# Attention and a two-layer expert on one core: expert products as three fp16 products instead of three fp32r products

## The chip, the cores and the metric

One NeuronCore of a Trainium2 chip runs the whole program. The metric is device microseconds of one execution, the median over runs. Its engines are called PE (TensorE, matmuls), DVE (VectorE), ACT (ScalarE), POOL (GpSimd) and SP (SyncE, which here issues every DMA). PEld is the weight load of a matmul, which overlaps PE.

## The reference

The program computes attention with a gated memory, and puts the result through an expert of two matrices. B, H, S, D are 4, 8, 576, 64; the expert is 512 by 2048 and back, for 2304 tokens.

```python
scores = scale * np.matmul(q, k.transpose(0, 1, 3, 2))      # causal mask, softmax -> a
local = np.matmul(a, v)
q_p = phi(q)                                                # elu + 1
mem_out = einsum(q_p, M_prev) / (einsum(q_p, z_prev)[..., None] + 1e-06)
attn = g * mem_out + (1 - g) * local                        # g = sigmoid(beta)
x = attn.transpose(0, 2, 1, 3).reshape(B * S, H * D)
h = x @ w_in                                                # w_in, w_out are float64
g = h * np.cos(h)
return (g @ w_out).astype(np.float32)
```

## The kernel before

**Tokens.** The 2304 tokens are nine chunks of 256. Chunk 0 is the first 64 rows of all four batches; its attention is done in four small pieces (`small_pair`). The rest comes in five attention jobs (`prm["jobs"]`): row blocks 1 and 2 of batch 0, row blocks 3 and 4 of batch 0, then all four row blocks of batches 1, 2 and 3. A job runs over four pairs of heads (`heads`), and fills `x`, one tile of 128 by 512 for each row block. While a job runs, the expert works on the chunks that earlier jobs finished (`moe_chunk`). The last two chunks are left when attention ends.

**Attention.** For a pair of heads PE makes the scores (`scores`, L540, fp32, in two halves of the array), DVE takes them from PSUM with mask and row minimum (`least`, L551), ACT takes the exponential with its sum (`expo`, L558). Then the weights of the softmax have to be turned. In all jobs but the first `parts` does so: ACT or DVE writes an fp16 high part (L363 or L365, both are the helper `copy`), DVE an fp16 rest (L570), SP issues a DMA transpose (L574), and the product with the values (`local`, L712) is fp16: 3r+2 matmuls of 64 columns for row block r. For this the values are scaled to a power of two and split (`values`, L615 to L627 and the helpers). In the first job `plain` is set: PE turns the softmax in fp32 (`turned`, L585 and L587), one copy takes it from PSUM, and the product is fp32 (L703).

**Expert.** A chunk has eight units. `unit1` makes 256 columns of h for 256 tokens (tile `u`), `hidden` makes g from them, `unit2` adds their share to two accumulators `acc`. In chunk 0 all of it is fp32 (`split` is false). In the other eight chunks x, g and both matrices are each the sum of an fp32r high part and an fp32r rest (`xh`, `xl`, `gh`, `gl`, `weight_high`, `weight_low`, or both in one tile, `wide_both`), and a product is three products: a `unit1` of 24 matmuls of 256 columns (L914), a `unit2` of 12 matmuls of 512 columns (L958). `emit_xT` turns x with four PE transposes for each of two tiles (L886); ACT rounds the high part out of PSUM (L897), DVE subtracts the rest. `hidden` is a chain ACT (L937), DVE (L939), ACT sine (L941), DVE (L943), ACT `gh` (L363), POOL or DVE `gl` (helper `sub`, L373).

**Weights.** `load_w` rebuilds a float32 tile from the two halves of float64 with POOL, ACT and DVE steps. When chunk 0 has used a tile for the last time, `split_w` splits it: ACT the high part (L504), DVE the rest (L511).

**Order.** Nothing runs in the order in which it is written. Each step is an `Op` with the engines that may do it, a cost, and a priority in `prm`; `Plan.forward` gives every engine one list of steps from these numbers, and the program holds each engine's steps in that order. There is one PSUM bank `mm` (transposes, memory products and sums of values share it), two for `S`, `u` and `acc` each, one for `pv`. A `w` tile has two buffers; two `s` tiles for each row block hold the softmax of the two heads of a pair.

Of the kernel before, what the change touches and what calls it, by code (L numbers as in the profile page):

```python
# [275 lines left out]
def dve(n, wide=False):  # L276
    return 65 + n / (1.92 if wide else 0.96)
# [15 lines left out]
def kernel(  # L293
# [33 lines left out]
    gate = sb.tile([128, 6, H], F32, name="gate")  # L327
    ig, il, ils = gate[:, 3, :], gate[:, 4, :], gate[:, 5, :]
# [161 lines left out]

    def split_w(key, prio, used):
        if len(w_split) >= prm["wide"] and wide:
            ph = pl = wide.pop(0)
        else:
            ph, pl = [(places or last).pop(0) for part in range(2)]
# [12 lines left out]
        def low(e):
            if ph != pl:
                wl[key] = sb.tile([128, 512], F32R, tag=pl, name=f"{pl}_low")  # L510
            eng[e].tensor_tensor(out=wl[key], in0=wv[key], in1=wh[key].bitcast(F32), op=ALU.subtract)  # L511

        o = Pp(some({"ACT": act(512, False), "DVE": dve(512, True), "Pool": pool(512)}, "hi_on"), high, prio,
               after=[w_ready[key], *left_by.get(ph, list)()])
        w_ready[key] = Pp(some({"DVE": dve(512), "Pool": 1240}, "lo_on"), low, prio, after=[o, *left_by.get(pl, list)()])
        w_split.append(key)
        done = [*used, w_ready[key]]
        left_by[w_place[key]] = lambda: done
        places.append(w_place[key])
# [652 lines left out]
```

## Time and profile before

| | |
|---|---|
| runs | 579.73 us median of 3 (579.24 to 580.37) |
| span of the profiled execution | 578.5 us |
| PE, PEld busy | 98%, 81% |
| DVE, ACT, POOL busy | 70%, 70%, 28% |
| chain that ended last | PE 81% of it, ACT 7%, DMA 5%, DVE 3% |

The profiled execution's time is its span of 578.5 us; the median of the runs is 1.2 us above it. A matmul's record is longer than its place on PE, because matmuls are pipelined: what one costs is the distance from its start to the next one's, which is read from a row of several that follow each other.

### The profile page before, as it was taken

The numbers are of one execution on the slowest core, as the hardware profiler recorded it, in microseconds if no ns is written. First come the engines' busy times: TensorE is split into PE (matmuls) and PEld (weight loads), VectorE is DVE, ScalarE is ACT, GpSimd is POOL, SyncE is SP. The second block draws the span as 40 slices with busy tenths as digits, with TensorE's granted clock in tenths as the row PEclk, the third lists the DMA queues.
The fourth block names the chain that finished last, engine by engine and source line by source line (L and its number), as shares of the span: only waits on it lengthen the run. The fifth ranks groups of instructions, "written<-read, shape, count | busy, mean of one in ns | idle before, by whom it ended". The sixth has DMA issues, their size and how long they took to land.

```text
span 578.5 us, 12276 instructions
## 1 busy us (share of the span) xinstructions
PE 567.5 (98%) x4453; PEld 468.6 (81%) x4453; DVE 402.3 (70%) x1292; ACT 407.2 (70%) x872; POOL 160.1 (28%) x159
## 2 busy tenths in 40 slices
PE   8899999999999999999999999999999999999997
PEld 5677657688888788788977988888879999989995
DVE  4999788989989899889758855868698421321320
ACT  4997788898898897769657946968788532433432
POOL 2232330145225213115140311441213112222112
PEclk9999999999999999999999999999999999999999
DMA  8877773696644985485509810727056100000101
GB/s 277 286 228 236 241 231 98 122 200 139 140 97 99 182 160 114 92 168 143 81 0 191 168 31 1 164 76 150 1 103 125 31 1 19 19 0 1 38 0 37
DMA packets 113165, 64.96 MB, mean 112 GB/s; under 512 B 95952, under 2 KB 101584, under 8 KB 113104
## 3 DMA queue, kind: packets, MB, share of 16 engines
q1 hardware_dynamic: 113104, 64.18, 46.7%
q8 instruction: 35, 0.57, 0.4%
q14 instruction: 26, 0.21, 0.1%
HBM read 36.37 MB, written 4.72 MB: 71 GB/s over the span
## 4 chain that ended last, share of the span: by engine, by line
PE 81%; ACT 7%; DMA 5%; DVE 3%; issue 2%; SPq 1%; POOL 0%; ACTq 0%; POOLq 0%; DVEq 0%
PE u L914 32%; PE acc L958 31%; PE S L540 7%; PE pv L712 5%; DMA t<-p 2%; PE pv L703 2%; PE mm L669 2%; ACT s L558 2%; PE mm L886 1%; DMA ws<-in_w_in 1%; DVE p L570 1%; DMA q<-in_qk 1%; SPq L379 1%; ACT p L363 1%; ACT x L689 1%
## 5 line engine op out<-in xcount | busy, mean ns | idle before, releaser
L373 POOL TENSOR_TENSOR gl<-w,gh 128x512 fp32r<-128x512 f32 x64 | 84.7, 1325 | 249.7 <-ACT gh L363 175.2
L914 PE MATMUL u<-xh,weight_high 128*128 128x256 f32 x416 | 119.4, 287 | 1.0 <-DVE w L943 1.0
L914 PE MATMUL u<-xl,weight_high 128*128 128x256 f32 x416 | 115.9, 279 | 0.0
L914 PE MATMUL u<-xh,weight_low 128*128 128x256 f32 x416 | 115.7, 278 | 0.0
L939 DVE SCALAR_TENSOR_TENSOR w<-w,u 128x512 f32<-128x512 int32 x72 | 49.1, 684 | 84.7 <-ACT w L937 68.3
L958 PE MATMUL acc<-weight_high,gh 128*128 128x512 f32 x240 | 97.8, 407 | 0.0
L958 PE MATMUL acc<-weight_low,gh 128*128 128x512 f32 x240 | 94.4, 393 | 0.0
L958 PE MATMUL acc<-weight_high,gl 128*128 128x512 f32 x240 | 94.1, 392 | 0.0
L570 DVE SCALAR_TENSOR_TENSOR p<-s,p 128x64 f16<-128x64 f32 (+1 forms) x224 | 83.1, 414 | 6.2 <-ACT p L363 5.6
L914 PEld LDWEIGHTS u<-xh,weight_high 128*128 128x128 f32 x416 | 78.3, 188 | 6.5 <-issue 2.5
L558 ACT ACTIVATE s<-s,nb 128x448 f32<-128x448 f32 (+3 forms) x128 | 77.6, 610 | 5.9 <-DVE nb L551 5.6
L914 PEld LDWEIGHTS u<-xl,weight_high 128*128 128x128 f32 x416 | 78.3, 188 | 1.4
L914 PEld LDWEIGHTS u<-xh,weight_low 128*128 128x128 f32 x416 | 78.5, 189 | 0.0
L937 ACT ACTIVATE w<-u 128x512 int32<-128x512 f32 x72 | 42.4, 592 | 47.3 <-PE u L914 28.0
L363 ACT ACTIVATE gh<-w 128x512 fp32r<-128x512 f32 x56 | 35.2, 628 | 49.0 <-PE acc L958 40.6
L551 DVE CUSTOM_DVE_ANT_0 s<-S,mask 128x320 f32<-128x320 f32 (+3 forms) x128 | 65.5, 532 | 4.1 <-PE S L540 3.8
L943 DVE TENSOR_TENSOR w<-w,u 128x512 f32<-128x512 f32 x64 | 43.5, 683 | 22.4 <-ACT w L941 22.3
L540 PE MATMUL S<-stq 64*128 64x320 f32 (+4 forms) x320 | 55.6, 455 | 0.0
L941 ACT ACTIVATE w<-w 128x512 f32<-128x512 f32 x72 | 45.0, 629 | 14.8 <-DVE w L939 14.0
L958 PEld LDWEIGHTS acc<-weight_high,gh 128*128 128x128 f32 x240 | 45.1, 188 | 11.2 <-issue 2.7
L958 PEld LDWEIGHTS acc<-weight_low,gh 128*128 128x128 f32 x240 | 45.1, 188 | 10.1
L958 PEld LDWEIGHTS acc<-weight_high,gl 128*128 128x128 f32 x240 | 45.2, 188 | 7.5
(123 smaller groups left out, 1037.0 us busy)
## 6 DMA issues: line engine op xcount, KB each, us to landing
ws<-in_w_in SPq DMA_DIRECT2D x16, 512.0 KB, 5.4
ws<-in_w_out SPq DMA_DIRECT2D x16, 512.0 KB, 4.2
stq<-in_qkp SPq DMA_DIRECT2D x12, 544.0 KB, 4.2
stv<-in_vk SPq DMA_DIRECT2D x16, 320.0 KB, 3.3
out<-w SPq DMA_DIRECT2D x16, 256.0 KB, 2.2
t<-p SPq DMA_TRANSPOSE x112, 3.2
mz<-in_mzp SPq DMA_DIRECT2D x20, 66.0 KB, 2.6
stq<-in_qkp SPq DMA_DIRECT2D x4, 288.0 KB, 3.6
```

Source lines behind the costliest of these rows:

```text
L363: nc.scalar.activation(out=out, in_=in_, func=ACTF.Copy, scale=scale)
L373: lambda e: eng[e].tensor_tensor(out=out, in0=in0, in1=in1, op=ALU.subtract), prio, port=kw.pop('port', True), **kw)
L540: nc.tensor.matmul(out=sv.ap[:, c:c + n], lhsT=pair.ap[p, qs], rhs=pair.ap[p, k0:k0 + n], start=True, stop=True)
L551: return P.op({"DVE": dve(n) + 10}, lambda e: nc.vector.tensor_tensor_reduce(out=st.ap[:, k0:k0 + n], in0=sv.ap[:, c:c + n], in1=mk, scale ...
L558: return P.op({"ACT": act(W, False, 2)}, lambda e: nc.scalar.activation(out=st.ap[:, 0:W], in_=st.ap[:, 0:W], func=ACTF.Exp, scale=-1.0, b ...
L570: Pp({"DVE": dve(n)}, lambda e, c=c, n=n, to=to: nc.vector.scalar_tensor_tensor(out=pt.ap[:, to:to + n], in0=sa[:, c:c + n], scalar=PSCALE ...
L914: nc.tensor.matmul(out=u.ap[:, f, :], lhsT=a[:, cs:cs + 128], rhs=x, start=(n == 0), stop=(n == len(terms) - 1))
L937: P.op({"ACT": act(512)}, lambda e: nc.scalar.activation(out=wi, in_=u.ap, func=ACTF.Copy, bias=0.25), ep, r=[u], w=[w])
L939: P.op({"DVE": dve(512)}, lambda e: nc.vector.scalar_tensor_tensor(out=wv, in0=wi, scalar=0.25, in1=u.ap, op0=ALU.subtract, op1=ALU.subtra ...
L941: P.op({"ACT": act(512, False)}, lambda e: nc.scalar.activation(out=wv, in_=wv, func=ACTF.Sin, scale=-TWO_PI_BELOW), ep, w=[w], table="sin")
L943: P.op({"DVE": dve(512)}, lambda e: nc.vector.tensor_tensor(out=wv if split else views[0], in0=wv, in1=u.ap, op=ALU.mult), ep, r=[u], w=[w ...
L958: nc.tensor.matmul(out=acc[b].ap, lhsT=a, rhs=w, start=(i == 0 and f == 0 and n == 0), stop=(2 * i + f == NF - 1 and n == len(terms) - 1))
```

## The change

Five things change.

1. **Products.** x, g and both matrices are split into fp16 parts instead of fp32r parts, high and rest in one tile (`weight_both`). A product is still three products. In the program an fp16 matmul is a LDWEIGHTS and a MATMUL; an fp32r one is a MATMUL alone that loads its own weights.
2. **Scales.** fp16 needs scales. For each of eight groups of four weight tiles PE makes the Gram matrix of their upper halves (16 matmuls of 128 columns in bf16, read with a step of two), DVE takes its trace, PE adds it over partitions (one matmul of one column), DVE makes a power of two (`powers`). `factors` is run once when all eight are there. For x ACT takes sums of squares (one for each tile), PE adds them, DVE makes the scale. The scales enter as an operand per partition in `split_w`, in `hidden` and in `finish`.
3. **x.** No PE transposes for the eight split chunks. DVE scales x in place, ACT or DVE writes the fp16 high part, DVE or POOL the rest, SP issues one DMA transpose of eight 128 by 128 blocks for each tile.
4. **First job.** `plain` is 0: the first job goes through `values`, `parts` and the fp16 product as the others do.
5. **Order.** New costs and priorities in `prm` and in the `P.op` calls, hence a new order on all engines.

The counts of instructions that differ most, from the two programs:

| | before | after |
|---|---|---|
| expert products of split chunks | 1536 fp32r of 256 columns, 768 of 512 | 1536 fp16 of 256, 768 of 512 |
| first job's products with values | 40 fp32 | 104 fp16 |
| first job's PE transposes | 40 | 0 |
| PE transposes of x, split chunks | 64 | 0 |
| Gram matmuls; sums over partitions of one column | 0; 16 | 128; 44 |
| `gl` on POOL, on DVE | 64, 0 | 15, 49 |
| ACT table loads | 52 | 60 |
| DMA transposes of softmax, of x | 112, 0 | 128, 16 |
| instructions of DVE, ACT, POOL | 1294, 714, 164 | 1459, 782, 106 |

The diff, cut to its core:

```diff
+    def powers(prio, src, q, sc, r=(), a=(), after=()):
+        bank, xn = P.buf("mm"), P.buf("xn")
+        if r:
+            for b, x in enumerate(r):
+                def squares(e, x=x, to=xn.ap[:, b:b + 1]):
+                        nc.scalar.activation(out=junk_a, in_=x.ap, func=ACTF.Square, accum_out=to)
+        else:
+            def gram(e):
+                blocks = [x.bitcast(BF16)[:, 2 * c + 1:2 * c + 256:2] for x in src() for c in range(0, 512, 128)]
+                for n, x in enumerate(blocks):
+                    nc.tensor.matmul(out=bank.ap[:, 0:128], lhsT=x, rhs=x, start=(n == 0), stop=(n == len(blocks) - 1))
+            def trace(e):
+                    nc.vector.tensor_tensor_reduce(out=junk_d, in0=bank.ap[:, 0:128], in1=ident, scale=1.0,
+                                                   scalar=2.0**-100, op0=ALU.mult, op1=ALU.add, accum_out=xn.ap[:, 0:1])
+        def total(e):
+            for b in range(nb):
+                nc.tensor.matmul(out=bank.ap[:, 128:129], lhsT=ones.to_broadcast([128, 128]), rhs=xn.ap[:, b:b + 1],
+                                 start=(b == 0), stop=(b == nb - 1))
+        def go(e):
+            nc.vector.tensor_scalar(out=q.bitcast(I32), in0=bank.ap[:, 128:129].bitcast(I32), scalar1=1, scalar2=0x7F800000,
+                                    op0=ALU.logical_shift_right, op1=ALU.bitwise_and)
+            nc.vector.tensor_scalar(out=sc.bitcast(I32), in0=q.bitcast(I32), scalar1=-1, scalar2=204 << 23,
+                                    op0=ALU.mult, op1=ALU.add)
+    def factors(prio):
...
     def split_w(key, prio, used):
-                wh[key] = sb.tile([128, 512], F32R, tag=ph, name=f"{ph}_high")
-                nc.scalar.copy(out=wh[key], in_=wv[key])
-            eng[e].tensor_tensor(out=wl[key], in0=wv[key], in1=wh[key].bitcast(F32), op=ALU.subtract)
+            both = sb.tile([128, 1024], F16, tag=place, name=f"{place}_both")
+                nc.scalar.activation(out=wh[key], in_=wv[key], func=ACTF.Copy, scale=s)
+            eng[e].scalar_tensor_tensor(out=wl[key], in0=wv[key], scalar=s, in1=wh[key], op0=ALU.mult, op1=ALU.subtract)
...
     def emit_xT(prio, xbs, split):
-            bufs = [P.buf("xh"), P.buf("xl")]
+            xt, cs = P.buf("xT"), P.buf("cs")
+            o = powers(prio, None, cs.ap[:, 5:6], cs.ap[:, 6:7], r=xbs, a=[cs])
+                Pp({"DVE": dve(512, True, 1), "Pool": pool(512) + 65}, lambda e, xb=xb: eng[e].tensor_scalar(
+                    out=xb.ap, in0=xb.ap, scalar1=s, scalar2=1.0, op0=ALU.mult, op1=ALU.mult), prio, w=[xb], after=[o])
+                copy(hv, xb.ap, 512, prio, on=prm["xh_on"], r=[xb], w=[half])
+                sub(lv, xb.ap, hv, 512, prio, on=prm["xl_on"], r=[xb, half], w=[half])
+                P.op({"SP": 1200}, lambda e, b=b, half=half: nc.sync.dma_start_transpose(out=xt.ap[:, b], in_=half.ap), prio,
+                     r=[half], a=[xt], move=140.0 * 8, lead=-230.0)
...
     def hidden(ep, i, u, split, cs=None):
+            P.op({"ACT": act(512, extra=1)}, lambda e: nc.scalar.activation(
+                out=wi, in_=u.ap, func=ACTF.Copy, scale=d, bias=0.25), ep, r=[u, cs], w=[w])
+            P.op({"DVE": dve(512, extra=1)}, lambda e: nc.vector.scalar_tensor_tensor(
+                out=wv, in0=u.ap, scalar=d, in1=wi, op0=ALU.mult, op1=ALU.subtract), ep, r=[u, cs], w=[w])
+                out=wv, in_=wv, func=ACTF.Sin, scale=TWO_PI_BELOW, bias=quarter), ep, w=[w], table="sin", after=[o_const])
+                out=wv, in0=wv, scalar=ej, in1=u.ap, op0=ALU.mult, op1=ALU.mult), ep, r=[u], w=[w], after=w_fac)
...
-    "plain": 1,
+    "plain": 0,
-    "hi_on": ('ACT',),
-    "lo_on": ('DVE',),
+    "gram": 240.0,
```

How the new order moves things, at three places.

PE in chunk 0, the stretch in which it makes the first fp32 units and the first job's attention (`mm` is the shared bank, `s` a softmax tile, `t` a turned one, `stv` and `v` values). Before:

```order
L914 MATMUL u_129<-s_82,weight_val 128x256 x2
L914 MATMUL u_129<-s_86,weight_val 128x256 x2
L585 MATMUL mm_133<-ident,s_75 64x128
L587 MATMUL mm_133<-ident,s_75 128x128
...
L669 MATMUL mm_133<-mz_70,e_69 128x132 x2
L703 MATMUL pv_132<-stv_67,t_84 128x64 x3
L703 MATMUL pv_132<-stv_67,t_80 128x64 x2
L540 MATMUL S_130<-stq_65 128x320
```

After:

```order
L997 MATMUL u_142<-s_88,weight_val 128x256 x2
L997 MATMUL u_142<-s_92,weight_val 128x256 x2
L518 LDWEIGHTS weight_val
L518 MATMUL mm_146<-weight_val 128x128
...
L787 MATMUL pv_145<-v_78,t_82 128x64
L997 MATMUL u_141<-s_88,weight_val 128x256 x2
L997 MATMUL u_141<-s_92,weight_val 128x256 x2
L532 LDWEIGHTS ones
L532 MATMUL mm_146<-xn_118,ones 128x1
```

The transposes of the softmax and the fp32 products with values are gone; Gram products and sums over partitions stand between the fp32 units, and they use the bank `mm`.

DVE in the job of batch 1, around one unit of the expert. Before, where `gl` of the unit is on POOL's list:

```order
L939 SCALAR_TENSOR_TENSOR w_103<-w_103,u_129 128x512
L551 ISA s_78,nb_114<-S_130,mask 128x320
L551 ISA nb_114 128x1
L679 RECIPROCAL r_122<-r_122 128x4
L551 ISA s_74,nb_114<-S_130,mask 128x192
L551 ISA nb_114 128x1
L685 TENSOR_TENSOR x_98<-mm_133,r_122 128x128
L685 TENSOR_TENSOR x_99<-mm_133,r_122 128x128
```

After:

```order
L1024 SCALAR_TENSOR_TENSOR w_111<-u_142,cs_117,w_111 128x512
L1028 SCALAR_TENSOR_TENSOR w_110<-w_110,wfac,u_141 128x512
L620 ISA s_93,nb_127<-S_143,mask,nb_127 128x64
...
L620 ISA s_88,nb_128<-S_144,mask 128x448
L620 ISA nb_128 128x1
L380 TENSOR_TENSOR gl_114<-w_110,gh_112 128x512
L726 SCALAR_TENSOR_TENSOR e_75<-stq_71,e_75 128x512
```

`gl` has come onto DVE's list, among the scores of the next pair of heads, and both DVE steps of the unit read a scale per partition.

PE where the chunks of the last job begin. Before, PE turns x between products:

```order
L914 MATMUL u_128<-xl_101,wide_both 128x256
L914 MATMUL u_128<-xh_100,wide_both 128x256
L886 MATMUL mm_133<-ident,x_94 128x128 x4
L958 MATMUL acc_127<-weight_high,gh_104 128x512
L958 MATMUL acc_127<-weight_high,gl_106 128x512
```

After:

```order
L997 LDWEIGHTS weight_both
L997 MATMUL u_142<-xT_109,weight_both 128x256
L532 LDWEIGHTS ones
L532 MATMUL mm_146<-xn_120,ones 128x1
L532 LDWEIGHTS ones
L532 MATMUL mm_146<-xn_120,ones 128x1
L997 LDWEIGHTS weight_both
```

PE now only adds the two sums of squares there; the turning has gone to SP's list, as two DMA transposes for each chunk.

## Rows read from the trace of the kernel before

**Rows 1.** The page, parts 1, 2: engines' busy time; granted clock in 40 slices.

```profile
PE 567.5 (98%) x4453; PEld 468.6 (81%) x4453; DVE 402.3 (70%) x1292; ACT 407.2 (70%) x872; POOL 160.1 (28%) x159
...
PEclk9999999999999999999999999999999999999999
```

**Rows 2.** Busy time by stage: stretch, length, PE, PEld, DVE, ACT, POOL, granted clock, DMA.

```profile
20.00:40.00 20.00, 17.23 (x108) 13.93 (x108) 19.99 (x64) 19.02 (x51) 6.66 (x8) 1.00 0.73 234
...
0.00:30.00 30.00, 24.36 (x218) 17.71 (x219) 21.35 (x109) 22.39 (x71) 7.59 (x24) 1.00 0.83 278
30.00:110.00 80.00, 79.97 (x363) 54.19 (x362) 70.68 (x185) 66.63 (x144) 20.23 (x25) 1.00 0.63 197
110.00:300.00 190.00, 189.43 (x1751) 157.96 (x1750) 161.96 (x557) 156.73 (x339) 62.89 (x54) 1.00 0.63 127
300.00:465.00 165.00, 164.03 (x1438) 140.41 (x1437) 120.41 (x403) 121.76 (x255) 43.58 (x37) 1.00 0.44 91
465.00:578.50 113.50, 109.66 (x692) 98.37 (x690) 27.93 (x43) 39.72 (x66) 25.85 (x20) 1.00 0.04 15
```

**Rows 3.** Chain that ended last, in order of time: start, length, line, matmuls.

```profile
29.84 1.73 PE u L914 x8
...
38.19 1.68 PE pv L703 x10
...
221.96 1.12 PE pv L712 x38
...
513.00 2.75 PE u L914 x24
...
560.91 13.77 PE acc L958 x60
```

**Rows 4.** Timeline of PE: a pair of bf16 matmuls and some fp32 transposes.

```profile
18.10 0.38 PE L398 MATMUL acc<-mask 128*128 128x256 bf16 x2
...
23.71 0.50 PE L886 MATMUL mm<-ident,x_first 128*128 128x128 f32 x3
```

**Rows 5.** Groups by line, PE: count, busy time, mean ns, idle before.

```profile
L886 PE MATMUL mm<-ident,x 128*128 128x128 f32 x64 | 10.0, 278 | 0.1
L618 PE MATMUL mm<-va,ones 128*128 128x1 bf16 x16 | 2.8, 177 | 0.0
L398 PE MATMUL acc<-mask 128*128 128x256 bf16 x8 | 1.6, 276 | 0.0
```

**Rows 6.** Groups by line, DVE and POOL.

```profile
L373 POOL TENSOR_TENSOR gl<-w,gh 128x512 fp32r<-128x512 f32 x64 | 84.7, 1325 | 249.7 <-ACT gh L363 175.2 <-issue 20.4 <-DVE gh L365 18.3
L570 DVE SCALAR_TENSOR_TENSOR p<-s,p 128x64 f16<-128x64 f32 (+1 forms) x224 | 83.1, 414 | 6.2 <-ACT p L363 5.6
L943 DVE TENSOR_TENSOR w<-w,u 128x512 f32<-128x512 f32 x64 | 43.5, 683 | 22.4 <-ACT w L941 22.3
L685 DVE TENSOR_TENSOR x<-mm,r 128x128 f32<-128x128 f32 x36 | 8.7, 283 | 0.2
L598 DVE TENSOR_SCALAR sm<-sm,vs 128x4 f32<-128x4 f32 (+1 forms) x32 | 7.7, 250 | 0.7 <-ACT s L558 0.4
L365 DVE TENSOR_SCALAR gh<-w 128x512 fp32r<-128x512 f32 x8 | 3.4, 420 | 0.2
L621 DVE TENSOR_SCALAR vs<-mm 128x1 int32<-128x1 int32 x16 | 2.4, 151 | 2.0 <-PE mm L618 1.9
```

**Rows 7.** Groups by line, ACT.

```profile
L363 ACT ACTIVATE gh<-w 128x512 fp32r<-128x512 f32 x56 | 35.2, 628 | 49.0 <-PE acc L958 40.6 <-DVE w L943 7.0 <-PE mm L618 1.2
L941 ACT ACT_TABLE_LOAD x26 | 33.4, 1283 | 0.4
L558 ACT ACTIVATION_READ_ACCUMULATOR s<-s,nb 128x1 f32 x128 | 24.5, 191 | 0.0
L689 ACT ACTIVATE x<-mm,r 128x64 f32<-128x64 f32 x56 | 12.8, 312 | 3.5 <-DVE r L679 3.4
```

**Rows 8.** DMA issues: median us from issue to landing of the DMA transposes.

```profile
t<-p SPq DMA_TRANSPOSE x112, 3.2
```

More of the change, by code (lines that the diff above doesn't have):

```diff
@@ L491, in split_w @@
     def split_w(key, prio, used):
[L492 to L495, printed above, removed]
+        place = (places or last).pop(0)
+        o, j = (0, key[1]) if key[0] == "i" else (1, key[1] // 4)
+        s = wsc[:, o, j:j + 1]
         def high(e):
-            if ph == pl:
-                both = sb.tile([128, 1024], F32R, tag=ph, name=f"{ph}_both")
-                wh[key], wl[key] = both[:, 0:512], both[:, 512:1024]
-            else:
-                wh[key] = sb.tile([128, 512], F32R, tag=ph, name=f"{ph}_high")
-            if e == "ACT":
-                nc.scalar.copy(out=wh[key], in_=wv[key])
-            else:
-                eng[e].tensor_scalar(out=wh[key], in0=wv[key], scalar1=1.0, scalar2=1.0, op0=ALU.mult, op1=ALU.mult)
@@ new lines, in split_w @@
+        if (o, j) not in w_scale:
+            keys = [("o", 4 * j + n) if o else ("i", j, n) for n in range(4)]
+            w_scale[o, j] = powers(prio, lambda: [wv[k] for k in keys], wq[:, o, j:j + 1], s,
+                                   after=[w_ready[k] for k in keys])
+        h = Pp(some({"ACT": act(512, False, 1), "DVE": dve(512, True), "Pool": pool(512)}, "hi_on"), high, prio,
+               after=[w_scale[o, j], *left_by.get(place, list)()])
+        w_ready[key] = Pp({"DVE": dve(512, extra=1)}, low, prio, after=[h])
@@ L519, in split_w @@
         places.append(w_place[key])
-    w_split, users = [], {}
+        if len(w_scale) == 8 and not w_fac:
+            w_fac.append(factors(prio))
+    w_scale, w_fac, users = {}, [], {}
     def weights(j, prio):
@@ L541, in prod @@
                                      start=True, stop=True)
-        P.op({"PE": 194 + sum(4 * mm(n) for _, _, n, _ in pieces)}, prod, prio, kind="s", r=[pair], w=svs)
+        P.op({"PE": sum(2 * max(125, 62 + n / 1.2) for _, _, n, _ in pieces)}, prod, prio, kind="s", r=[pair], w=svs)
         return svs
@@ L1121 @@
     "hi_on": ('ACT',),
-    "lo_on": ('DVE',),
+    "gram": 240.0,
+    "ahead": [],
+    "pl_on": ('DVE', 'Pool'),
+    "xh_on": ('ACT', 'DVE'),
+    "xl_on": ('DVE', 'Pool'),
     "clamp_on": ('DVE', 'Pool'),
```

174 lines of the change are left out of this document (105 added, 69 removed).

## The prediction

> **What bounds the kernel now.** I read the page's busy times first, then the same by stage, then the chain in order of time, then the groups by line for prices. PE is busy 567.5 of 578.5 us, with the granted clock in the top tenth in every slice [rows 1]. By stage [rows 2] PE has work all through 30 to 465 us; it idles 5.6 us in the first 30 us, some 1.6 us between 30 and 465, and in the drain after the last product. So the time is a sum of PE's places, and an edit pays where it makes that sum smaller. The second thing to see is how far the others are. Attention's last product with values ends at 464.6 us. Up to 465 us DVE is busy 374.4 us and ACT 367.5 (the first four stages added), 81% and 79%; after it 27.9 and 39.7 of 113.5 us. In the stage 30 to 110 us DVE is at 88%. And in the stretch 20 to 40 us DVE is at 99.9% and ACT at 95%: there, and only there for so long, PE stands still for 14% of the time. A fuller DVE is what PE can come to wait for.
>
> **The change part by part, PE.** Prices are distances from start to start [rows 3].
> *Products of 256 columns.* fp32r: 2.75/24 = 0.1146 us. What fp16 takes is not in the trace. The nearest rows: fp16 matmuls of 64 columns with a weight load each stand 1.12/38 = 0.0295 us apart, which is 64 columns at 2.4 GHz (0.0267) and 0.0028 more; that makes 0.1095 for 256 columns. Two bf16 matmuls of 256 columns take 0.38 us together where one is 0.276 long [rows 4, 5], so 0.104 apart. I take 0.1095: 1536 x 0.0051 = 7.8 us less. If fp16 is no faster than fp32r it is 0.
> *Products of 512 columns.* fp32r: 13.77/60 = 0.2295 us. In the same way fp16 is 0.2133 + 0.0028 = 0.2161: 768 x 0.0134 = 10.3 us less, again 0 at the other end.
> *First job.* Its fp32 products go: 80 records of 1.68/10 = 0.168 us, 13.4 us. Its 40 transposes go at (0.50 - 0.278)/2 = 0.11 us each [rows 4, 5], 4.4 us. 104 fp16 matmuls come, 104 x 0.0295 = 3.1 us, and four sums of values. Net 14.3 us less.
> *x.* 64 transposes at 0.11: 7.0 us less; they now stand outside PE.
> *Gram.* 128 matmuls of 128 columns come. By the fp16 rows that is 128/2.4 + 2.8 = 0.056 us, by the fp32 transposes of 128 columns 0.11; the operands are read with a step of two, so it may be either: 7.2 to 14.1. I take 0.06, near the 16-bit row: 7.7 us. 24 more one-column sums at 0.1 (a record of 0.177 [rows 5], less its overlap): 2.4 us.
> Switches between 32-bit and 16-bit work move from the products to the fp32 parts around them; I count them as nothing, within 4 us either way.
> Sum for PE: -7.8 - 10.3 - 14.3 - 7.0 + 7.7 + 2.4 = -29.3 us. If nothing else were late, the span would be 578.5 - 29.3 = 549.2 us.
>
> A rule of the Trainium skill would make more of it. In the trace every kind of 16-bit matmul costs at least its columns at 2.4 GHz, 0.0295 us for 64 and 0.104 or more for 256 [rows 3 to 5]. The page "TensorE: Matmul & The Clock Gate", section "Back-to-back issue gap", gives for a stream of pairs of weight load and matmul about 81 ns at 128 columns and 131 ns at 512. By it the Gram products are 10.4 us by estimate, inside my bounds, but the 512-column products would lose 768 x (0.2295 - 0.131) = 76 us by estimate. The row of 64 columns speaks against it; it is the last rival.
>
> **DVE, ACT and the others.** Where does the work go that PE gave up? For DVE up to the end of attention, counted in the new order: 30 of the 49 `gl` that come from POOL, at 0.683 as for other 128x512 steps of two tensors, 20.5 us (POOL took 1.325 [rows 6]); a scale per partition read in some 125 steps, priced by two small steps, with one (0.250) and without (0.151), 12.5; 32 more rests of the first job's softmax at 83.1/224 = 0.37, 11.9; 11 scalings of x at 0.42, 4.6; some 15 steps of the values that POOL had, 8; some 60 small steps of the scales at 0.15, 9; less 16 memory steps that ACT takes over at 0.283, 4.5. That is 62 us of records; records of neighbours overlap (224 of 0.414 are 92.7 us, but 83.1 busy [rows 6]), so 56: DVE has 430 us to do.
> ACT gets 8 table loads at 1.283, 12 sums of squares at 0.628 + 0.191, 32 memory steps at 0.312, some 130 scale operands at 0.1, some 36 high parts and values, less 18 copies of the first job [rows 7]: about 50 us, 418 in all.
> How long does PE give them? After the last product with values PE has, in the order before, 420 + 258 products and 16 transposes, 109.1 us; in the new order 408 + 252, 99.1 us. So 10.0 of the 29.3 us are gained in the tail, and attention would have to end at 464.6 - 19.3 = 445 us. That asks 430/445 = 97% of DVE and 94% of ACT. Bounds: at 100%, nothing is lost; at the 88% of the stage 30 to 110 us, 430/0.88 = 489, 44 us. I take 95%, nearer to what the stretch 20 to 40 us shows: 453 us, **8 us** of waiting that PE cannot make up, since its work in the tail has no slack.
> The transposes of x take the place of four matmuls and two steps. A DMA transpose of a softmax tile lands 3.2 us after its issue [rows 8]; with squares, sum, scale, high part and rest ahead of it the new chain is some 9 us. Units of earlier chunks hide it: in the new order some 8 us of them stand between the sum of squares of the last job's first chunk and its first product. I cost it at nothing; uncovered it is 2 to 4 us at each of the chunk boundaries, inside the range. SP gets 32 more DMA transposes; queued behind one that waits are the next loads of q, k and v.
>
> **The forecast.** 549.2 + 8 = 557.2 us for the profiled execution; the median stands 1.2 us above the span, so **558.5 us**.
>
> **Rivals.**
> *PE alone sets it.* DVE and ACT keep up: 549 to 552, with the median's 1.2 us 550.5. For it: the 99.9% of the stretch 20 to 40 us. Against: PE waited there.
> *DVE holds attention longer, but not past the gain.* At 92%: 430/0.92 = 467, 22 us late: 549.2 + 22 + 1.2 = 572. For it: DVE, ACT, PE and the DMA transposes wait on each other for each pair of heads, and both helpers are now nearly full at once.
> *Slower.* The same mechanism at the 88% of 30 to 110 us: attention ends at 489 instead of 445, 44 us late: 549.2 + 44 + 1.2 = 594. It decides from the point at which attention ends 29.3 us late, at 474 us, that is when DVE gets less than 430/474 = 91% out of this order. For it: no stage of more than 20 us shows a share that high; against: before, DVE had no cause to be fuller, because PE was the bound.
> *fp16 gains nothing over fp32r.* Then 18.1 us come back: 576.5. For it: no fp16 product of 256 or 512 columns is in the trace; against: the bf16 pair.
> *The rule of 131 ns.* 558.5 less some 65: 493.
>
> **How the numbers follow.** Forecast (553 to 565) 0.42; PE alone (541 to 553, if the switches also pay) 0.25; DVE longer 0.14; fp16 no gain 0.04; slower 0.12; the rule 0.01; about the same 0.02. The range leaves out the slower case, the rule and little else: 543 to 580. A difference of 0.2%, 1.2 us, is about what a measurement can tell from no change here. Faster: 0.42 + 0.25 + 0.14 + 0.04 + 0.01 = 0.86; same 0.02; slower 0.12.
>
> **What would show it.** Products: 24 `u` in about 2.63 us and 60 `acc` in 12.97 in the tail; if not, the terms 7.8 and 10.3 are wrong. Gram: 16 matmuls in about 1 us; above 1.8 the term is. First job and x: no PE time but 13 matmuls in 0.38 us for each head. DVE: busy 94 to 97% up to the last attention product, which should end near 453 us; PE idle before products with values or scores, released by DVE, ACT or a DMA of `t`, of some 8 us more than before. If PE waits for `xT` or for `ones` products instead, the chain of x was not covered. A granted clock below the top tenth would make every price here wrong.

## The result and the profile after

The changed kernel takes **570.92 us** (median of 4 runs, 569.56 to 572.09); the kernel before took 579.64 (579.24 to 580.37) beside it. The ratio is 0.9839, 95% interval 0.9816 to 0.9861: 1.6% faster, where the forecast was 3.65% (558.5 us). The profiled execution has a span of 570.4 us against 578.5. One execution of the run in experiment 5 that has the first job in fp32 is slow (693.94 us, at a granted clock of 0.757 where the other three have 0.994 to 0.997) and is left out of its median.

The page of the kernel after: busy time of each engine, and the granted clock in 40 slices; the rows of before are in [rows 1].

```profile
PE 541.0 (95%) x4529; PEld 367.4 (64%) x4529; DVE 454.0 (80%) x1457; ACT 452.6 (79%) x960; POOL 82.5 (14%) x101
...
PEclk9978999999999999998999999999999999999999
```

PE has 26.5 us less to do than before, but stands still for 570.4 - 541.0 = 29.4 us where it was 11.0. And the clock row, an unbroken line of nines before, has three slices below.

The same by stage (stretch, length, busy time of PE, PEld, DVE, ACT, POOL, granted clock, DMA share, GB/s), against [rows 2]:

```profile
0.00:30.00 30.00, 23.95 (x208) 17.22 (x208) 22.57 (x110) 23.96 (x83) 8.04 (x26) 0.96 0.92 292
30.00:110.00 80.00, 74.06 (x474) 51.72 (x475) 73.25 (x228) 70.84 (x150) 22.72 (x30) 0.95 0.82 213
110.00:300.00 190.00, 177.38 (x1675) 119.43 (x1675) 173.77 (x605) 173.45 (x382) 39.95 (x36) 0.99 0.68 139
300.00:460.00 160.00, 159.59 (x1403) 109.09 (x1402) 135.52 (x435) 136.25 (x268) 11.81 (x10) 1.00 0.47 100
460.00:570.40 110.40, 105.99 (x774) 69.92 (x771) 48.91 (x83) 48.10 (x80) 0.00 (x0) 1.00 0.11 28
```

PE's new idle time lies between 30 and 300 us: 5.9 and 12.6 us in the two stages, where before it was 0.0 and 0.6. From 300 us on there is as little as before. In the same two stages DVE and ACT are the fullest: DVE 91.6% and 91.5%, ACT 88.6% and 91.3%.

Where the clock fell: the three stretches at half clock (1.2 GHz; the granted clock of the rows is 0.52 to 0.54), each behind what PE did just ahead of it.

```profile
24.16:27.57 3.41, 1.98 (x17) 1.57 (x16) 3.41 (x14) 3.41 (x12) 1.05 (x2) 1.00 1.25 368
27.57:34.40 6.83, 5.49 (x24) 4.04 (x24) 6.59 (x21) 5.75 (x19) 2.66 (x3) 0.52 1.08 194
44.64:48.05 3.41, 0.88 (x18) 0.73 (x16) 3.41 (x13) 2.39 (x5) 1.63 (x2) 1.00 0.76 258
48.05:51.46 3.41, 3.41 (x11) 2.58 (x10) 2.49 (x9) 1.26 (x3) 0.63 (x1) 0.54 0.99 262
263.10:266.50 3.40, 1.04 (x7) 0.55 (x5) 3.11 (x17) 3.40 (x13) 0.00 (x0) 1.00 1.17 125
266.51:269.92 3.41, 2.45 (x12) 1.77 (x13) 1.84 (x8) 1.58 (x5) 0.00 (x0) 0.54 0.89 176
```

Each follows a stretch in which PE had stood still for 1.4 to 2.5 of 3.4 us. In the slow stretches PE is busy 5.49 + 3.41 + 2.45 = 11.35 us; at full clock that work would take about half, so the dips cost some 5.7 us by estimate. So PE's busy time at full clock is 541.0 - 5.7 = 535.3 us, **32.2 less** than before's 567.5; 18.4 of it went into idle time and 5.7 into the clock, and 8.1 are left: the difference of the two spans.

What PE waited for from 20 to 300 us in the kernel after, the six largest (us in all, times, longest). `nb` is the row minimum of the scores, `vs` a scale of the values, `t` of L1039 and `w` are hidden values of the expert:

```profile
PE pv L787 <- DMA t<-p: 4.0, 3, 2.2
PE u L997 <- DMA xT<-x: 3.3, 2, 3.1
PE u L997 <- DVE t L1039: 2.5, 1, 2.5
PE S L609 <- DVE nb L620: 2.5, 3, 1.0
PE u L997 <- DVE w L1028: 2.1, 2, 1.7
PE mm L744 <- DVE vs L696: 1.5, 2, 1.0
```

No one cause leads. Two kinds of DMA transposes hold 7.3 us, single steps of DVE most of the rest.

### The profile page after: what moved, and what is told of

It reads as the page before. It is cut to its first block, busy times and chain, and to the rows that moved or that the text cites. A ratio compares the mean times of both kernels' runs of the same rounds, so it can differ in the third digit from the quotient of the medians.

```text
span 570.4 us, 12689 instructions
## 1 busy us (share of the span) xinstructions
PE 541.0 (95%) x4529; PEld 367.4 (64%) x4529; DVE 454.0 (80%) x1457; ACT 452.6 (79%) x960; POOL 82.5 (14%) x101
## 4 chain that ended last, share of the span: by engine, by line
PE 43%; ACT 20%; DVE 17%; DMA 13%; issue 5%; SPq 1%; POOL 0%; ACTq 0%; DVEq 0%; POOLq 0%
PE u L997 20%; PE acc L1051 17%; DMA t<-p 6%; DVE s L620 3%; PE pv L787 3%; ACT s L627 3%; DVE p L645 3%; DMA ws<-in_w_in 2%; ACT weight_both L570 2%; DMA xT<-x 2%; ACT p L370 2%; PE S L609 2%; ACT L627 2%; ACT w L1026 1%; DVE w L1028 1%
## 5 line engine op out<-in xcount | busy, mean ns | idle before, releaser
L997 PE MATMUL u<-xT,weight_both 128*128 128x256 f16 x1536 | 180.1, 274 | 6.0 <-DMA xT<-x 3.3
L997 PEld LDWEIGHTS <-weight_both 128*128 128x128 f16 x1536 | 148.7, 98 | 35.9 <-issue 8.2
L1051 PE MATMUL acc<-weight_both,gh 128*128 128x512 f16 x512 | 163.4, 379 | 0.0
L1051 PE MATMUL acc<-weight_both,gl 128*128 128x512 f16 x256 | 97.0, 379 | 0.0
L645 DVE SCALAR_TENSOR_TENSOR p<-s,p 128x64 f16<-128x64 f32 (+4 forms) x256 | 86.1, 376 | 6.6 <-ACT p L370 6.0
L1051 PEld LDWEIGHTS <-gh 128*128 128x128 f16 x512 | 50.0, 98 | 58.5 <-issue 4.4
L627 ACT ACTIVATE s<-s,nb 128x320 f32<-128x320 f32 (+3 forms) x128 | 77.4, 607 | 0.8 <-DVE x_first L858 0.3
L1024 DVE SCALAR_TENSOR_TENSOR w<-u,cs,w 128x512 f32<-128x512 f32 x64 | 47.6, 744 | 28.1 <-ACT w L1022 27.9
L609 PE MATMUL S<-stq 64*128 64x448 f32 (+4 forms) x320 | 59.3, 463 | 2.5 <-DVE nb L620 2.5
L1026 ACT ACTIVATE w<-w,quarter 128x512 f32<-128x512 f32 x64 | 45.7, 719 | 14.8 <-DVE w L1024 14.3
L370 ACT ACTIVATE p<-s 128x320 f16<-128x320 f32 (+3 forms) x100 | 48.3, 501 | 9.5 <-DMA t<-p 9.2
L787 PEld LDWEIGHTS <-t 128*128 128x128 f16 x1216 | 40.3, 98 | 13.1 <-issue 5.2
L609 PEld LDWEIGHTS S<-stq 64*128 64x128 f32 x320 | 29.4, 189 | 22.5 <-issue 10.9
```

The lines of the kernel that those rows point to most:

```text
L370: nc.scalar.activation(out=out, in_=in_, func=ACTF.Copy, scale=scale)
L609: nc.tensor.matmul(out=sv.ap[:, c:c + n], lhsT=pair.ap[p, qs], rhs=pair.ap[p, k0:k0 + n], start=True, stop=True)
L627: return P.op({"ACT": act(W, False, 2)}, lambda e: nc.scalar.activation(out=st.ap[:, 0:W], in_=st.ap[:, 0:W], func=ACTF.Exp, scale=-1.0, b ...
L645: Pp({"DVE": dve(n)}, lambda e, c=c, n=n, to=to: nc.vector.scalar_tensor_tensor(out=pt.ap[:, to:to + n], in0=sa[:, c:c + n], scalar=PSCALE ...
L787: nc.tensor.matmul(out=pv.ap[:, 64 * i:64 * i + 64], lhsT=got[r].ap[:, block, :], rhs=vals.ap[:, part, h % 2, 64 * j:64 * j + 64], start=( ...
L997: nc.tensor.matmul(out=u.ap[:, f, :], lhsT=a[:, cs:cs + 128], rhs=x, start=(n == 0), stop=(n == len(terms) - 1))
```

## The experiments

Six of the twelve kernels keep the order of every engine as the changed kernel has it and change only what an instruction reads, how many columns it covers, or whether it is there (two of them with a few clears on POOL at the start); three add filling matmuls to that order, one moves a step from ACT to POOL, and two have a new order made by the planner. Times are medians; ratios are to the kernel before on the same chip, the changed kernel's own being 0.9839. Differences in us are between medians of runs on several chips; by the ratios most come out within 0.7 us of them (the first filled run: 2.6 in place of 4.1).

**1. Is it DVE's load?** The low parts of weights and of hidden values on 64 of 512 columns:

```diff
-            eng[e].scalar_tensor_tensor(out=wl[key], in0=wv[key], scalar=s, in1=wh[key], op0=ALU.mult, op1=ALU.subtract)
+            eng[e].scalar_tensor_tensor(out=wl[key][:, 0:64], in0=wv[key][:, 0:64], scalar=s, in1=wh[key][:, 0:64], op0=ALU.mult, op1=ALU.subtract)
...
-            sub(views[1], wv, views[0], 512, ep, on=prm["gl_on"], r=[w, bufs[0]], w=[bufs[1]])
+            P.op({"DVE": dve(512), "Pool": 190 + 2.05 * 512}, lambda e: eng[e].tensor_tensor(
+                out=views[1][:, :, 0:32], in0=wv[:, :, 0:32], in1=views[0][:, :, 0:32], op=ALU.subtract), ep, port=True, r=[w, bufs[0]], w=[bufs[1]])
```

> The changed kernel in its own order, with less work for DVE and POOL: the low parts of the expert weights (32 steps) and of the hidden values (64 steps) are made on 64 of 512 columns, and the products with low parts read the high parts in their place, so the output is not the reference's. Between 30 and 300 us that takes some 32 x 0.5 + 7 x 0.55 = 20 us off DVE's 247. Theory LOAD (DVE and ACT, both over 88% busy between 30 and 300 us, set PE's 18.6 us of idle time there): most of it goes, and the two dips of the granted clock in this stretch with it; 553 to 560 us against 570.9. Theory LATENCY (single chains over a DMA transpose set it): the waits for DMA and for the small steps stay; 566 to 571.

Measured: 570.83 us, 0.9837 (0.981 to 0.9863): nothing gained. The two stages in this kernel:

```profile
30.00:110.00 80.00, 75.42 (x476) 52.63 (x477) 68.36 (x230) 71.47 (x152) 22.46 (x30) 0.94 0.82 215
110.00:300.00 190.00, 178.23 (x1674) 119.57 (x1673) 160.63 (x603) 173.30 (x381) 28.82 (x36) 0.97 0.68 138
```

DVE is busy 229 us of these 270 in place of 247, ACT is as full as before, PE's idle time is 16.4 instead of 18.5 us and the clock even lower, so the little idle time that was won stands against more time at half clock. This part of DVE's load, taken off by itself, gains nothing.

**2. Is it the transposes by DMA?** First the products of x read a constant, then those with values too:

```diff
+                    x = [ident.bitcast(F16)] * 2 if split else x
                     terms += [(wh[key], x[0]), (wh[key], x[1]), (wl[key], x[0])] if split else [(wv[key], x[0])]
...
-                    nc.tensor.matmul(out=pv.ap[:, 64 * i:64 * i + 64], lhsT=got[r].ap[:, block, :],
+                    nc.tensor.matmul(out=pv.ap[:, 64 * i:64 * i + 64], lhsT=ident.bitcast(F16)[:, 0:128],
```

> The changed kernel in its own order, but the products of x with the weights read a constant tile in place of xT, so none waits for x's DMA transposes (these still run; the output is not the reference's). Theory LATENCY: the wait of 3.13 us at 264 us and the dip of the clock behind it (3.41 us at half clock, up to 1.7 us) go: 565.5 to 568. Theory LOAD: PE meets the next late scores or values instead; 569 to 571. The term of the prediction that put x's new chain at nothing is wrong by what this run gains.

> As the run without the wait for xT, and besides the products with values read a constant in place of t, so no product waits for any DMA transpose (the transposes still run; the output is not the reference's). Theory LATENCY: the waits for t of 1.57 and 2.24 us go too, 6.9 us of idle time in all with up to 1.7 of clock: 560 to 564. Theory LOAD: DVE and ACT still have the same work in front of scores and sums, so PE waits for them: 567 to 571.

Measured: without the wait for xT 569.85 us, 0.9823 (0.9797 to 0.9849), so 1 us and no difference that can be told from none. The largest single wait of the kernel after is gone; these are left (waits of PE from 20 to 300 us in this run):

```profile
PE pv L787 <- DMA t<-p: 3.4, 3, 1.8
PE S L609 <- DVE nb L620: 2.5, 3, 1.0
...
PE mm L744 <- DVE vs L696: 1.8, 2, 1.7
```

The 1.7 us for `vs` are new and stand at 269 us, 5 us behind the place where the wait for xT had been. More of what was won stands against a lower clock:

```profile
30.00:110.00 80.00, 75.76 (x476) 52.80 (x477) 74.84 (x231) 72.20 (x155) 23.93 (x30) 0.94 0.78 215
110.00:300.00 190.00, 181.12 (x1693) 122.72 (x1692) 174.26 (x606) 173.74 (x382) 39.94 (x36) 0.97 0.67 139
```

PE's idle time in the two stages is 13.1 us, 5.4 less than in the kernel after, but PE spends 20.4 us of this execution at half clock, in five stretches, where it was 13.65 in three. This execution has the lowest clock of the run's four (0.980 to 0.991), so not all of that need be the edit's doing. Without any wait for a DMA transpose: 565.9 us, 0.9752 (0.9722 to 0.9783), 5.0 us gained, between the two theories. That is two thirds of the 7.3 us that PE waited for transposes in the kernel after; those of x alone are the smaller part.

**3. Is it the clock?** Matmuls on constants where PE stands still; their results are overwritten:

```diff
+    def fill(n):
+        warm(P.groups["acc"][0][0][:, 0:256], n)
...
+            fill(13 if pr == 3 else 0)
...
+                fill(0 if b else 10)
...
+                if not split and (i, f) == (2, 0):
+                    fill(20)
+                if split and (chunk, i, f) == (3, 0, 0):
+                    warm(u.ap[:, 0, :], 27)
```

> The changed kernel with 70 bf16 matmuls of 256 columns on constants (0.107 us each) put at four places where PE stands still: 13 ahead of the wait at 25 us, 10 ahead of the one at 30, 20 ahead of the one at 45 and 27 ahead of the one at 264. Their results are overwritten; nothing is left out. Theory CLOCK (the three stretches at half clock, 13.65 us in all, follow from these waits and cost about half of the busy time in them, 6 us): the granted clock stays at 1.00 there and the time falls by 4 to 7 us, to 564 to 567. Theory NO CLOCK (half clock lies in stretches in which PE would have waited anyway): 570 to 573.

Measured: 566.85 us, 0.9794 (0.975 to 0.9839), in the range of theory CLOCK, but the interval reaches up to the changed kernel's own ratio. The trace shows 60 of the 70 (the ten at 30 us were left out by a loop variable that is read late), and the clock still fell from 31.7 to 38.5 us, behind the wait that was not filled. With 11 there in place of ten, and 7 and 8 more at two other places:

> The changed kernel with filling matmuls at all the places named for the first filled run, the ten at 30 us among them, which that run lacked (its trace shows 60 of the 70): 13 at 25 us, 7 and 11 between and behind the transposes at 29 us, 20 at 45, 27 at 264 and 8 ahead of one pair of score products; nothing is left out. Theory CLOCK: the stretch at half clock that the first filled run still had from 31.7 to 38.5 us goes as well (3.3 us of 566.9): 562 to 565. Theory NO CLOCK: what is left are waits for others, which this does not shorten: 566 to 569.

Measured: **565.51 us**, 0.9736 (0.9722 to 0.9751). This kernel computes everything, and its interval lies below the changed kernel's: it beats both. Windows of the kernel after, then of this one:

```profile
20.00:40.00 20.00, 15.08 (x91) 11.11 (x91) 17.32 (x65) 15.59 (x51) 5.72 (x8) 0.83 1.05 258
40.00:60.00 20.00, 17.47 (x118) 13.29 (x118) 18.33 (x54) 16.61 (x36) 7.59 (x10) 0.91 0.93 239
260.00:280.00 20.00, 15.84 (x169) 12.25 (x170) 16.21 (x66) 16.05 (x45) 5.63 (x5) 0.91 0.86 165
```

```profile
20.00:40.00 20.00, 17.73 (x134) 13.78 (x133) 19.34 (x68) 17.12 (x57) 6.46 (x9) 1.00 1.01 273
40.00:60.00 20.00, 19.64 (x153) 15.68 (x153) 19.70 (x58) 17.01 (x35) 7.60 (x10) 1.00 0.96 230
260.00:280.00 20.00, 19.91 (x220) 16.38 (x221) 17.38 (x65) 17.59 (x46) 4.54 (x4) 1.00 0.85 180
```

What is left at half clock in this kernel, and its page:

```profile
129.70:133.10 3.40, 3.40 (x18) 2.37 (x17) 3.40 (x10) 3.40 (x8) 1.16 (x1) 0.51 0.90 138
```

```profile
PE 545.6 (97%) x4615; PEld 372.8 (66%) x4615; DVE 456.6 (81%) x1457; ACT 452.6 (80%) x960; POOL 83.1 (15%) x101
```

Work that computes nothing bought 5.4 us, half a microsecond less than theory CLOCK asked and more than NO CLOCK allowed. That it is the clock, and not shorter waits, shows in the sum: PE stands still for 564.4 - 545.6 = 18.8 us, and the 86 filling matmuls take 86 x 0.107 = 9.2, together 28.0 where PE's idle time was 29.4. The dips cost 1.7 us in place of 5.7, so some 4.0 of the 6.0 us between the two spans are the clock. A dip does not always reach the end: of the changed kernel's four executions the one with the lowest clock (0.978) is the second fastest (570.31 us).

**4. Is it ACT's load, or both engines'?**

```diff
-                nc.scalar.activation(out=wh[key], in_=wv[key], func=ACTF.Copy, scale=s)
+                nc.scalar.activation(out=wh[key][:, 0:64], in_=wv[key][:, 0:64], func=ACTF.Copy, scale=s)
-            out=a, in_=a, func=ACTF.Prelu, scale=2.0**-112, alpha=-2.0**32), prio, w=[t])
+            out=a[:, 0:64], in_=a[:, 0:64], func=ACTF.Prelu, scale=2.0**-112, alpha=-2.0**32), prio, w=[t])
-                nc.scalar.activation(out=spare[:, 0:n + 1], in_=stv.ap[:, 0:n + 1], func=ACTF.Abs, accum_out=sums.ap)
+                nc.scalar.activation(out=spare[:, 0:65], in_=stv.ap[:, 0:65], func=ACTF.Abs, accum_out=sums.ap)
...
-                out=pt.ap[:, to:to + n], in0=sa[:, c:c + n], scalar=PSCALE, in1=hi[:, c:c + n], op0=ALU.mult,
+                out=pt.ap[:, to:to + 64], in0=sa[:, c:c + 64], scalar=PSCALE, in1=hi[:, c:c + 64], op0=ALU.mult,
```

(The last pair is DVE's, in the second of the two runs only; there the rests of the hidden values are cut as in experiment 1.)

> The changed kernel in its own order with less work for ACT alone: the high parts of the expert weights, the step between loading and joining the two halves of a weight, the sums of the values and the sums of squares of x run over 64 columns in place of 512 (or 256 to 640), and the products read the low parts where they read the high parts, so the output is not the reference's. Between 30 and 300 us that takes 32 x 0.36 + 25 x 0.37 + 14 x 0.45 + 8 x 0.35 = 30 us off ACT's 244. Theory ACT (the chain of the changed kernel runs over ACT almost without a break from 65 to 130 us): PE's idle time of 18.5 us between 30 and 300 us falls to 10 or less, 560 to 565 us. Theory LATENCY (single waits, for transposes by DMA and for small steps on DVE): 568 to 572.

> As the run with a light ACT, and DVE relieved too: the rests of the softmax tiles and of the hidden values are made on 64 columns each (the tiles are cleared once at the start), some 25 us less for DVE between 30 and 300 us; the output is not the reference's. Theory LOAD of both engines together: with 12% off ACT and 10% off DVE, idle time of PE between 30 and 300 us falls below 6 us and the granted clock stays up, 553 to 560 us. Theory LATENCY: as without the second relief, 566 to 571.

Measured: ACT alone 566.96 us, 0.978 (0.9744 to 0.9815), just clear of the changed kernel's 0.9816 to 0.9861; both 561.55 us, 0.9676 (0.9644 to 0.9709). The two stages, first with ACT light, then with both:

```profile
30.00:110.00 80.00, 75.56 (x483) 52.48 (x483) 76.72 (x238) 57.86 (x162) 23.55 (x29) 0.96 0.79 216
110.00:300.00 190.00, 180.18 (x1702) 122.83 (x1701) 175.58 (x598) 161.49 (x374) 40.17 (x36) 0.97 0.66 138
```

```profile
30.00:110.00 80.00, 75.21 (x484) 52.18 (x485) 75.12 (x247) 58.24 (x163) 22.77 (x30) 0.96 0.82 222
110.00:300.00 190.00, 181.67 (x1734) 124.67 (x1733) 151.77 (x593) 162.68 (x376) 27.63 (x36) 0.98 0.67 137
```

Relieving DVE in experiment 1 gave nothing, ACT alone 4.0 us (while DVE filled up to 96% in the first stage), both together 9.4. That fits two engines that are full together, where one that is relieved runs into the other. It is not shown to the end, since DVE's relief is not the same: beside the rests of the hidden values, experiment 1 cut the low parts of the weights, and this run cuts the rests of the softmax, which stand ahead of the transposes of `t`; no run relieves DVE of these without ACT. PE's waits for `t` are not what became shorter (4.3 us with ACT light, 3.7 with both). Neither theory's figures were met: 9.4 us is less than LOAD asked (11 to 18), and idle time in these stages is still 13.1 us. PE's idle time is only 4.7 us less over the whole span; the rest is a shorter busy time of PE with the same products.

That busy time is waiting too. PE's order is the same in both kernels, so its matmuls can be compared one by one, outside the slow stretches: 39 give way to the next at least 0.04 us sooner (5.9 us in all), ten later (1.6 us), and all the others together change by 0.04 us. A matmul that comes a little late starts while the record of the one ahead still runs, and the profile calls that time busy.

**5. Do savings on PE count where it waits anyway?** The scales of the weights given as constants, so that no Gram product is computed:

```diff
-            P.op({"PE": prm["gram"] * len(after)}, gram, prio, w=[bank], after=after, kind="v")
+            P.op({"PE": prm["gram"] * len(after)}, lambda e: None, prio, w=[bank], after=after, kind="v")
...
+        nc.gpsimd.memset(wq, 2.0**-41)
+        nc.gpsimd.memset(wsc, 16.0)
```

> The changed kernel in its own order, but the scales of the weights are constants: the 128 Gram products (6.9 us of PE by the trace of the changed kernel), their traces, the 8 sums and the steps that make scales of them are left out, so the output is not the reference's, and no split of a weight waits for a scale. If only PE's own time counts: 570.9 - 7.3 = 563.5 us. If the chain from Gram product over DVE, the sum and DVE again to the first high part holds more (the wait of 0.76 us at 71 us, the bank that is held meanwhile): 557 to 562. If PE waits in that stage anyway and the Gram products lie in time that it had: 568 to 571.

Measured: 570.71 us, 0.9828 (0.9791 to 0.9866), no difference that can be told from none: the third case. The stage that lost the Gram products:

```profile
30.00:110.00 80.00, 68.47 (x348) 44.00 (x348) 71.41 (x200) 72.28 (x153) 22.77 (x29) 0.97 0.81 214
```

and what PE waited for from 20 to 300 us in this run:

```profile
PE mm L746 <- DVE vs L698: 6.4, 5, 2.4
PE u L999 <- DVE t L1041: 3.5, 1, 3.5
```

PE now stands still for 11.5 us of this stage, 5.6 more, and the median does not move: PE comes earlier to the same steps of DVE and waits there (6.4 us for `vs`, 1.5 before this edit). Between 30 and 110 us PE's own time is not what sets the pace. (The execution shown is the fastest of this run, 567.96 us, and the one shown of the changed kernel its slowest, 572.09: what the edit gains overall is told by the medians alone.)

The other way round: the first attention job on PE in fp32 again.

```diff
-    "plain": 0,
+    "plain": 1,
```

> The changed kernel with one part undone: the first attention job computes its products with values in fp32 from tiles that TensorE transposes, as before (the flag for it is set again; the order is made anew from the same numbers, since the operations differ; nothing is left out). Theory SUM (PE's own time counts wherever it lies, as the prediction's term of 14.3 us for this part has it): 570.9 + 14.3 = 585 us, 582 to 588. Theory STAGE (up to some 130 us PE waits for DVE, ACT and DMA, so work put back on PE there fills time in which it stood still, and DVE and ACT get rid of the rests): 568 to 576.

Measured: 577.14 us, 0.9935 (0.9915 to 0.9955): 6.2 us slower, between the two theories. PE's idle time between 30 and 110 us fell to 3.1 us and its clock stayed at 1.00:

```profile
30.00:110.00 80.00, 76.90 (x448) 55.51 (x446) 71.06 (x195) 66.70 (x145) 20.89 (x26) 1.00 0.59 189
```

Where the 6.2 us lie is seen from the last product with values and what stands behind it, here and in the changed kernel:

```profile
465.14 1.27 PE L787 MATMUL pv<-v,t 128*128 128x64 f16 x38
466.41:577.07 110.66, 106.86 (x725) 70.31 (x722) 48.23 (x78) 47.90 (x77) 0.00 (x0) 1.00 0.08 25
```

```profile
466.80:570.38 103.58, 99.19 (x664) 64.47 (x662) 44.80 (x73) 44.78 (x72) 0.00 (x0) 1.00 0.09 26
```

Attention ends at 466.4 us, no later than in the changed kernel (466.8); the tail is 7.1 us longer. The new order has put some 60 products of the expert behind the end of attention that stood ahead of it (46 of 256 columns, 13 of 512, 7.8 us by the prices of the tail). So part of the fp32 work filled time in which PE had stood still, and part of it pushed other products back; what the part is worth by itself, without a new order, can't be told from this run.

**6. Is it the new order?**

```diff
-    "w0": -6.075636,
+    "w0": -21.959923814923563,
-    "wdt": 87.40036,
+    "wdt": 25.426382740430082,
-    "t0": 3.32467,
+    "t0": 57.56913966923671,
...
```

> All operations of the changed kernel, but the order made with the numbers of the kernel before (start and spacing of jobs, units, weights and softmax steps; biases of the engines; the costs in the planner stay those of the change). Theory ORDER (the new numbers bring the first job and the weights so close together that PE runs dry between 30 and 130 us): with the old spacing PE's idle time there shrinks and the time is 560 to 568. Theory WORK (PE has less to do there and the other engines more, in any order): the idle time lies elsewhere but is as long or longer, 571 to 585.

Measured: 578.16 us, 0.9962 (0.9932 to 0.9992): theory WORK. Its engines, and its last product with values:

```profile
PE 538.7 (94%) x4529; PEld 368.8 (64%) x4529; DVE 423.4 (74%) x1367; ACT 434.1 (75%) x924; POOL 192.4 (33%) x205
```

```profile
470.96 1.27 PE L787 MATMUL pv<-v,t 128*128 128x64 f16 x38
```

All the arithmetic of the change with the old numbers is worth 0.4%; the other 1.2% came with the new numbers. They are more than a spacing: with the old ones `gl` stays on POOL (64 steps, 15 in the changed kernel), and DVE and ACT have 31 and 19 us less to do, most of DVE's behind 300 us. PE stands still for 36.4 us, 7.0 more than in the changed kernel, and attention ends at 472.2.

**7. Do the causes add?** Experiments 2, 3 and 4 together:

> The changed kernel with the three causes taken away together: ACT and DVE relieved as in the run with both light, no product waits for a DMA transpose, and 59 bf16 matmuls of 256 columns on constants fill PE's idle time at 25, 30 and 45 us; the output is not the reference's. If the causes are separate, their gains add: 570.9 - 9.4 - 5.0 - 4.1 = 552.4, so 550 to 555, next to the 550.5 that the prediction gave for PE alone. If they are one cause seen three times (the same waits, reached in three ways): no better than the best of them, 558 to 562.

Measured: 555.81 us, 0.957 (0.9545 to 0.9595): 15.1 us of the 18.5 that the sum asks, just outside the first case and clearly better than the second. So the causes are separate for the most part; 3.4 us are common to them. Attention ends at 451.4 us here:

```profile
450.08 1.27 PE L802 MATMUL pv<-v,ident 128*128 128x64 f16 x38
...
30.00:110.00 80.00, 78.16 (x518) 54.15 (x516) 77.61 (x247) 60.02 (x167) 23.11 (x29) 1.00 0.85 226
110.00:300.00 190.00, 185.01 (x1760) 126.84 (x1759) 154.09 (x605) 165.38 (x379) 27.64 (x36) 0.99 0.65 136
```

**8. Can POOL take the load?**

```diff
-            if e == "ACT":
-                nc.scalar.activation(out=wh[key], in_=wv[key], func=ACTF.Copy, scale=s)
+            if True:
+                nc.gpsimd.tensor_scalar(out=wh[key], in0=wv[key], scalar1=s, scalar2=1.0, op0=ALU.mult, op1=ALU.mult)
```

> The kernel with more filling matmuls, and besides the 32 high parts of the expert weights made on POOL in place of ACT (0.71 us each there, 22 us between 30 and 300 us; POOL's steps of 512 columns took 0.76 in the changed kernel and POOL is busy 62 of these 270 us); everything else stays in its order and nothing is left out. Theory LOAD (ACT and DVE are both nearly full between 30 and 300 us): the run with a light ACT gained 4.0 us by 30 us less of ACT, so 565.5 - 3 = 562.5, 561 to 564. Theory LATENCY or a port that POOL shares with DVE: POOL's steps come later in the chain of a weight or lengthen DVE's, 565 to 569.

Measured: 570.37 us, 0.9831 (0.9807 to 0.9854): 4.9 us slower than the filled kernel it was made from, and above the ranges of both theories. Its first stage, and the moved steps between 30 and 300 us:

```profile
30.00:110.00 80.00, 73.73 (x505) 52.38 (x503) 77.82 (x220) 57.75 (x127) 46.98 (x55) 1.00 0.83 214
```

```profile
L573 POOL TENSOR_SCALAR weight_both<-weight_val,wsc 128x512 f16<-128x512 f32 x32 | 29.5, 931 | 7.5 <-DVE wsc L543 5.2 <-PE mm L535 1.3
```

ACT is relieved as in experiment 4, but a step takes 0.93 us in place of 0.71, DVE is at 97%, and PE's idle time in this stage is 6.3 us where the filled kernel had 3.4. Load that is moved is not load that is gone.

## Why the prediction was right and wrong

*PE's terms: right.* From the chain of the kernel after (start, length), 24 products of 256 columns and 48 of 512 in the tail; and from its timeline of PE 16 Gram products with what follows them, and the last products with values:

```profile
553.62 2.62 PE u L997 x24
556.24 10.37 PE acc L1051 x48
```

```profile
43.71 1.08 PE L518 MATMUL mm<-weight_val 128*128 128x128 bf16 x16
44.63 0.54 PE L787 MATMUL pv<-v,t 128*128 128x64 f16 x13
47.70 3.18 PE L997 MATMUL u<-s,weight_val 128*128 128x256 f32 x8 [2.53 <-DVE t L1039]
...
465.53 1.27 PE L787 MATMUL pv<-v,t 128*128 128x64 f16 x38
```

0.109 and 0.216 us each where 0.1095 and 0.2161 were taken [rows 3 to 5]; the 16 Gram products start within 0.9 us, so 0.057 to 0.06 each. All terms together were to be -29.3 us; PE's busy time at full clock is 32.2 less. The rule of the Trainium skill ("TensorE: Matmul & The Clock Gate", "Back-to-back issue gap") doesn't hold here: the products of 512 columns stand 0.216 us apart, not 0.131.

*The tail: right.* -10.0 us were forecast. The last product with values ends at 465.53 + 1.27 = 466.8 us, so 103.6 us are left, where it was 578.5 - 464.6 = 113.9: -10.3. That is more than the whole gain.

*The 8 us of waiting: the step that failed.* Attention was to end at 453 us; it ended at 466.8, 2.2 us later than before, and all of the 19.3 us that were to be gained in it were lost. The term of 8 us was mis-sized: PE's idle time grew by 18.4 us and the clock took 5.7, **24.1 us** in all. The step added DVE's work up to the end of attention, 430 us, and divided it by 95%. The work was less: up to 460 us the stages add up to 405 us of DVE and 405 of ACT. By the step's own rule (405/0.95 = 426, before the 445 that PE alone allows) that would have asked for no waiting at all. What the runs showed in its place has three parts:
- The share was taken over the whole phase, where the weights' part of the work lies in its first 300 us. There DVE and ACT are at 91% each; relieving both gives 9.4 us, ACT alone 4.0, a part of DVE alone nothing (experiments 1 and 4). DVE's place on the path looks like one that it shares with ACT, and one engine's share can't show that.
- The chain of x was costed at nothing, with 2 to 4 us at a boundary if it was not covered. One boundary was not (3.13 us at 264 us); taken away, it gave 1 us, with the next late step 5 us behind it and more time at half clock. With the transposes of `t`, which the forecast left as they were, it is 5.0 us (experiment 2).
- The granted clock was named only as something that would make the prices wrong. It fell behind PE's waits, and the slow stretches cost some 5.7 us; filling the waits gave 5.4 back (experiment 3).

With the three taken away together attention ends at 451.4 us (experiment 7), near the 453 that was forecast with all the work left in.

*PE's savings as one sum.* The sum counts a microsecond of PE wherever it lies. In the tail it came back in full. Between 30 and 110 us it turned into idle time: the Gram products cost nothing there, and the first job's 14.3 us put back on PE cost 6.2, a new order included (experiment 5).

*The rivals.* "DVE longer" (572) came out nearest in time, and its reason, that DVE, ACT, PE and the DMA transposes wait on each other while both helpers are nearly full, agrees with experiments 2 and 4; its arithmetic (430 us at 92%) is not what happened. The deciding point of "slower", a DVE share below 91%, did not decide: DVE is at some 88% up to the end of attention, and the kernel is still faster.

*The order.* It was no term of its own. Without the new numbers hardly anything of the gain is there, and attention ends at 472.2 us (experiment 6).

What stays open: the 6.8 us of idle time that PE still has between 30 and 300 us in experiment 7, how much of the first job's 6.2 us is the order, and what relief of the softmax rests alone would gain.

## What to carry to other kernels

Take savings of the bounding engine stage by stage: they pay where that engine has nothing to wait for (here the tail, 10.3 us of 10.0 forecast), and turn into idle time in a stage in which two helpers are at 90% together, even though neither is full. Read the helpers' share in such a stage for both at once, and try relief of each and of both, the same steps each time. A saving can also move: see whether a stage became shorter or only handed its work to the next. Where new waits make the matrix engine stand still for a few microseconds, look at the granted clock behind them; 86 matmuls on constants in the gaps gave back 5.4 us here.

## What the runs showed of the hardware

- In the changed kernel the clock fell to the 1.2 GHz level behind stretches in which PE was busy for 0.88, 1.04 and 1.98 of 3.4 us, and stayed there for 3.41 or 6.83 us. In the profiled execution of the kernel before it did not fall, though PE stood still for 14% of 20 to 40 us there too [rows 2]. Where matmuls whose results nobody reads were put into the waits, it stayed at 1.00 (experiment 3).
- Bf16 matmuls with 128 columns and operands read in steps of two start 0.057 to 0.06 us apart, no more than twice the 0.0295 us of 64 columns of fp16 read in a row [rows 3]: here the step cost nothing that can be seen.
- The same scaling of 128x512 elements took 0.71 us on ACT and 0.93 on POOL, while DVE's low parts of the weights beside it became longer (0.825 us in the mean, 0.764 in the filled kernel without it).
